# Identity matmuls in two places of the head, and unit 1 as eight plain block products

## The chip, the cores and the metric

The kernel runs on one core of one Trainium2 chip. The metric is the device time of one execution in microseconds, as the median of repeated executions. TensorE multiplies; VectorE, ScalarE and GpSimdE do the elementwise work (GpSimdE does not read PSUM, the buffer in which TensorE sums); SyncE issues nearly all DMAs. In the profile they are PE (and PEld, its weight loads), DVE, ACT, POOL and SP.

## The reference

Packed attention, then a mixture of four experts, all in float32:

```python
scale = 1.0 / np.sqrt(q.shape[-1])
def sm_attn(qq, kk, vv):
    s = scale * np.matmul(qq, kk.transpose(0, 1, 3, 2))
    s = s - np.max(s, axis=-1, keepdims=True)
    a = np.exp(s)
    a = a / (np.sum(a, axis=-1, keepdims=True) + 1e-09)
    return np.matmul(a, vv)
p_packed = sm_attn(p, k, v)            # 8 batches, 8 heads, 32 packed rows of 64
out = sm_attn(q, p_packed, p_packed)   # 576 tokens per batch
...
p = domain_probs / (domain_probs.sum(-1, keepdims=True) + 1e-09)
for e in range(E):                     # 4 experts, x is 4608 x 512
    h = np.maximum(x @ w1[e], 0.0)     # 512 x 1024
    out += p[:, e:e + 1] * (h @ w2[e]) # 1024 x 512
```

## The kernel before

**Precision.** A float32 operand is split into a high part (a cast to the faster float32 format, usually on ScalarE) and a low part (the rest, a subtraction, usually on GpSimdE). A product is three matmuls: high by low, high by high, low by high. `hi_of` and `lo_of` (lines 154 to 160) make the two parts; a low part reads the high part, so it waits for the cast.

**Attention.** `pack_unit` gives the packed rows of a batch and half its heads: scores, softmax, transposes of the softmax by TensorE, the copies of these out of PSUM by ScalarE (tile `at`, lines 247 and 248), the products with v (tile `vt`), and the result `ppbd`. `tok_unit` and, for batch 0, `tok_halves` compute the token side: scores against `ppbd`, softmax on VectorE, and the transposed softmax as `xh` and `xl`. The values are folded into the first expert layer: `g_form` multiplies `ppbd` by w1 (tile `wraw`), and `ghl` is the result's high and low part.

**Experts.** The eight halves of experts (512 of 1024 hidden columns) are chunks. A unit is one batch and one chunk; `units` (line 408) lists 64, of which the first four are (chunk 0, batch 0), (chunk 1, batch 0), (chunk 1, batch 1), (chunk 0, batch 1). Four `mm1_group`s of 12 matmuls make a unit's hidden tiles as four blocks a11, a12, a21, a22 (hidden half by token half); VectorE applies the relu and the probabilities `pbt`. The second layer is a Strassen-like scheme: seven products of 12 matmuls, in the order of `ORDER`, of sums of blocks on the left (`sblk`, `ablk`, their operands `st`, `stl`) and sums of blocks of w2 on the right (`tt`, made by `t_form` from the raw tiles `rw0`, `rw1`). `s_operand` and `split` make the left operands, `product` multiplies and adds into seven accumulators `acc`, and `combine` gives the four output blocks once per batch.

**The head** (lines 686 to 729) interleaves the attention of batches 0 and 1 with chunk 0's `t_form` and unit 0's mm1 groups. Ten identity matmuls open it (`FIRST`), 23 more follow the second mm1 group (`IDLE`); their results are not read. `norm_probs` writes the normalized probabilities to DRAM and `load_probs` reads them back as `pbt`.

**What sets the order.** TensorE's order is fixed by dependencies that `on_pe` and `together` add; in the head `vq` and `gq` do the same for VectorE and GpSimdE, in the order of the code. ScalarE's order, and the rest, is set by a planner at build time, which places each instruction by its own estimate of when it can start; on the chip each engine then takes its instructions in that order. Four PSUM buffers `dbl` and ten `tt` buffers rotate. `t_store` writes the right operands of a chunk to DRAM, `t_load` brings them back.

Of the kernel before, what the change touches and what calls it, by code (L numbers as in the profile page):

```python
# [8 lines left out]
F32 = mybir.dt.float32  # L9
# [7 lines left out]
P = 128  # L17
# [17 lines left out]
ORDER = ["a11", "s3", "s1", "s2", "a22", "s4", "a12"]  # L35
NPROD = len(ORDER)
IDLE = 23
FIRST = 10


@with_exitstack
def attention_moe(ctx: ExitStack, tc: tile.TileContext, q, k, v, p, dp, w1, w2, out):
# [91 lines left out]
    def dbl():  # L134
        return ps_dbl.tile([P, 2, 512], F32, name="dbl")

    ident = const.tile([P, P], F32, name="ident")
# [281 lines left out]
    def split(u, name, psv):  # L419

        tag, bufs = ("stl", 1) if name == "a12" else ("st", 4)
        st = hpool.tile([P, 2, 2, HP], F32R, name=tag, bufs=bufs)[:, :, :, 0:HS]
        hi_of(st[:, 0], psv, nc.scalar)
        lo_of(st[:, 1], psv, st[:, 0], vec)
        blocks[u, "op", ORDER.index(name) if name in ORDER else name] = st

    def mm1_group(u, kh, c, idle=0):
# [35 lines left out]
        )  # L463
        if u == len(units) - 1:
            if c != kh:
                split(u, name, psv)
        elif name == "a21":
            add(held("s3"), blocks[u, "a11"], psv, ALU.subtract)
            add(psv, psv, blocks[u, "a22"], ALU.add)
            add(held("s2"), psv, blocks[u, "a11"], ALU.subtract)  # L470
            nc.scalar.copy(out=held("s1"), in_=psv)  # L471
            if (u, "a12") in blocks:
                add(held("s4"), blocks[u, "a12"], blocks[u, "s2"], ALU.subtract)
        elif name == "a12":
            if (u, "s2") in blocks:
                add(held("s4"), psv, blocks[u, "s2"], ALU.subtract)
            else:
                blocks[u, "a12"] = psv
            split(u, name, psv)
# [32 lines left out]

    def t_form(ch, first=False):

# [4 lines left out]
        }  # L519
        of = {"a11": "b11", "a12": "b21", "s4": "b22", "a22": "t4", "s1": "t1", "s2": "t2", "s3": "t3"}  # L520
        steps = (
            ("a11", "t1", "t3"), ("s3", "s1", "t2"), ("s2", "t4"), ("a22",), ("s4",), ("a12",),
        )
        how = {"t1": ("b12", "b11", "b11"), "t2": ("b22", "t1", "t1"), "t3": ("b22", "b12", "b12"), "t4": ("t2", "b21", "t2")}
        for names in steps:
            for name in names:
                if name in how:
                    continue
                t = wpool.tile([P, 2, 2, DH], F32R, name="tt", bufs=10)
                hi_of(t[:, 0], blk[of[name]], bpool if first and of[name][0] == "t" else bact)  # L530
                tt[ch, ORDER.index(name)] = t
            for name in names:
                if name in how:
                    x, y, place = how[name]
                    bpool.tensor_tensor(out=blk[place], in0=blk[x], in1=blk[y], op=ALU.subtract)
                    blk[name] = blk[place]
                else:
                    t = tt[ch, ORDER.index(name)]
                    lo_of(t[:, 1], blk[of[name]], t[:, 0], bpool)
            yield  # L540

    accs = {}

    def product(u, i):
# [17 lines left out]
        else:  # L562
            vacc.tensor_tensor(out=accs[b, i], in0=psv, in1=accs[b, i], op=ALU.add)

    def store(b, t, r, n, j0=0):
# [20 lines left out]
    def last_unit(u):  # L586

        sb, ch, b = units[u]
        right = {"b11": ORDER.index("a11"), "b21": ORDER.index("a12"), "b22": ORDER.index("s4"), "b12": "b12"}
        pss = {}  # L590
        for half, (left, r) in enumerate((("a11", 0), ("a22", 1), ("a21", 1), ("a12", 0))):
            st = blocks.pop((u, "op", ORDER.index(left) if left in ORDER else left))
            for n in range(2):
                t = tt[ch, right[f"b{left[2]}{n + 1}"]]
                if half < 2:
# [75 lines left out]
    with ExitStack() as first:  # L671
# [26 lines left out]
        raws = w1_load(0)  # L698
        drain(wavefront(packs[:2], 1))
        for i in (2, 3, 2, 3):  # L700
            next(packs[i])
        load_probs(0, 0)
        next(halves)
        vq.on = gq.on = True
        next(forms)
        next(halves)
# [3 lines left out]
        for gen in toks:  # L710
            next(gen)
        load_probs(1, 0)
        for gen in packs[2:]:
# [31 lines left out]
    GROUPS = {1: ((0, 0),), 3: ((1, 1),), 4: ((0, 1),), 6: ((1, 0),)}  # L745
    GROUPS_FIRST = {2: ((0, 0),), 3: ((1, 1),), 4: ((0, 1),), 6: ((1, 0),)}
    GROUPS_LATE = {3: ((0, 0),), 4: ((1, 1),), 5: ((0, 1),), 6: ((1, 0),)}
    FORM = {0: (0, 2, 3, 4, 5, 6), 2: (6,), 3: (0, 1, 2, 3, 4)}
    for kh in range(2):
        w2_load(1, kh, raw_tile)  # L750
    tsteps = nothing
    kind = None
    sums, late, back = nothing, False, second_batch()
    for u, (sb, ch, b) in enumerate(units):
# [23 lines left out]
        if fch is not None and u != 3 and not (u > 3 and odd):  # L778
            tsteps = t_form(fch)
        form_at = FORM.get(u, () if fch is None else (1, 2, 3, 4) if odd else (1, 4))  # L780
# [4 lines left out]
        if u == len(units) - 2:  # L785
            b12_form(ch, raw12)
        for i in range(NPROD):
            product(u, i)
            n = i + LA
            if n < NPROD:  # L790
                s_operand(u, n)
            else:
                n -= NPROD
                s_operand(u + 1, ORDER.index("a22") if n and u == len(units) - 2 else n)
            if i in gat:
# [24 lines left out]
            for _ in range((0, 0, 2, 2, 2, 1, 0)[i] if late else 1):  # L820
                next(sums, None)
            if u < 2 or sb == 0 and u > 3 and not odd:
                t_store(ch, i)
# [48 lines left out]
```

## Time and profile before

| | us |
|---|---|
| median of 3 runs | 1272.03 (1271.49 to 1273.53) |
| span of the profiled execution | 1274.3 |
| TensorE busy | 1255.3 (99%) |
| VectorE / GpSimdE / ScalarE busy | 927.9 / 735.9 / 496.0 |
| mean granted TensorE clock | 0.995 of full |
| start of product 0 of unit 0 | 42.71 |
| start of product 0 of unit 2 | 91.92 |

TensorE's busy time contains matmuls at half the clock and overlapping records, so 99% is not full use. The span runs from the first to the last instruction; the profiled execution's span is longer than the median of the timed runs by 2.3 us. Lines such as L118 and L126 are those of the helpers `mm` and `together`, L70 is that of the recorded VectorE and GpSimdE calls, and L87 and L156 those of ScalarE's copies and casts, so the tile names tell the groups apart.

### The profile page before, as it was taken

What the parts mean: (1) busy time and instruction counts of PE and PEld (TensorE: products, weight loads), DVE (VectorE), ACT (ScalarE), POOL (GpSimd) and SP (SyncE); (2) the same over time, 40 slices, a digit from 0 to 9 for tenths busy, and PEclk for the clock granted to TensorE, in tenths of its full rate; (3) what the DMA queues carried; (4) which work ended last, traced back from release to release, by engine and by line L of the source; (5) the groups of instructions that cost most, each with busy time, mean ns of one, the idle gap of its engine ahead of it and who ended that gap; (6) DMA issues with size and microseconds to landing.
All of it is one profiled execution on the core that took longest, in us unless ns stands there. A gap on an engine that the chain in (4) does not pass through costs nothing.

```text
span 1274.3 us, 27033 instructions
## 1 busy us (share of the span) xinstructions
PE 1255.3 (99%) x10798; PEld 1176.4 (92%) x10798; DVE 927.9 (73%) x1389; ACT 496.0 (39%) x847; POOL 735.9 (58%) x529
## 2 busy tenths in 40 slices
PE   7899999999999999999999999999999999999998
PEld 5789899999999999999999999999999999999998
DVE  6585667788876677788777676788877567767766
ACT  2455444354445243343235433243343533323331
POOL 3876887798684343454467353454557545445456
PEclk8899999999999999999999999999999999999999
DMA  9675665536466444554345555433455443444422
GB/s 328 225 252 195 229 214 203 183 136 204 166 214 214 148 159 131 193 158 166 123 154 177 184 180 174 153 115 126 159 159 178 159 135 116 129 152 159 126 67 75
DMA packets 86508, 213.98 MB, mean 168 GB/s; under 512 B 8816, under 2 KB 27632, under 8 KB 86384
## 3 DMA queue, kind: packets, MB, share of 16 engines
q1 hardware_dynamic: 85712, 212.11, 50.3%
q8 instruction: 86, 1.41, 0.5%
q14 instruction: 38, 0.31, 0.1%
q10 hardware_dynamic: 672, 0.15, 0.1%
HBM read 173.35 MB, written 38.87 MB: 167 GB/s over the span
## 4 chain that ended last, share of the span: by engine, by line
PE 91%; DMA 2%; DVE 2%; POOL 2%; issue 1%; ACT 1%; SPq 0%; DVEq 0%; POOLq 0%; ACTq 0%
PE dbl L118 85%; PE dbl L126 5%; POOL st L70 1%; DMA pnd<-ablk 1%; PE dbl L121 1%; DMA pbt<-pnd 1%; DVE a L70 1%; POOL tt L70 1%; DMA wraw<-in_w 0%; DMA rw<-in_w 0%; DVE dbl L70 0%; DVE sblk L70 0%; POOL acc L70 0%; DVE s L70 0%; POOL rw L70 0%
## 5 line engine op out<-in xcount | busy, mean ns | idle before, releaser
L118 PE MATMUL dbl<-st,tt 128*128 128x288 f32 x4608 | 667.1, 296 | 3.9 <-DVE ghl L70 1.8
L118 PEld LDWEIGHTS dbl<-st,tt 128*128 128x128 f32 x4608 | 624.5, 188 | 38.9 <-POOL st L70 21.2
L70 POOL TENSOR_TENSOR st<-sblk,st 128x576 fp32r<-128x576 f32 x252 | 364.8, 1458 | 438.4 <-ACT st L156 434.1
L118 PE MATMUL dbl<-xh,ghl 128*128 128x288 f32 x2048 | 413.6, 294 | 0.0
L70 DVE TENSOR_TENSOR acc<-dbl,acc 128x576 f32<-128x576 f32 x390 | 292.3, 750 | 92.9 <-PE dbl L118 90.5
L118 PEld LDWEIGHTS dbl<-xh,ghl 128*128 128x128 f32 x2048 | 328.1, 188 | 0.2 <-DVE ghl L70 0.2
L118 PE MATMUL dbl<-xl,ghl 128*128 128x288 f32 x1024 | 302.6, 296 | 2.9 <-POOL xl L70 1.7
L156 ACT CAST st<-sblk 128x576 fp32r<-128x576 f32 x252 | 164.0, 674 | 362.6 <-DVE sblk L70 290.9
L70 POOL TENSOR_TENSOR st<-ablk,st 128x576 fp32r<-128x576 f32 x128 | 187.0, 1461 | 47.8 <-ACT st L156 47.8
L118 PEld LDWEIGHTS dbl<-xl,ghl 128*128 128x128 f32 x1024 | 192.6, 188 | 5.2 <-POOL xl L70 2.6
L70 DVE SCALAR_TENSOR_TENSOR dbl<-dbl,pbt 128x576 f32<-128x576 f32 x128 | 97.8, 764 | 77.0 <-PE dbl L118 75.8
L70 DVE SCALAR_TENSOR_TENSOR ablk<-dbl,pbt 128x576 f32<-128x576 f32 x128 | 96.4, 753 | 66.1 <-PE dbl L118 62.2
L156 ACT CAST st<-ablk 128x576 fp32r<-128x576 f32 x128 | 86.1, 674 | 124.3 <-PE dbl L118 92.4
L118 PE MATMUL dbl<-stl,tt 128*128 128x288 f32 x780 | 114.6, 296 | 0.0
L118 PEld LDWEIGHTS dbl<-stl,tt 128*128 128x128 f32 x780 | 106.0, 188 | 0.2
L70 DVE TENSOR_TENSOR ghl<-dbl,ghl 128x512 fp32r<-128x512 f32 x128 | 85.1, 686 | 27.3 <-ACT ghl L156 27.3
L156 ACT CAST ghl<-dbl 128x512 fp32r<-128x512 f32 x128 | 72.3, 590 | 56.8 <-DVE ghl L70 52.2
L70 POOL TENSOR_TENSOR tt<-rw,tt 128x512 fp32r<-128x512 f32 x57 | 74.3, 1320 | 18.4 <-ACT tt L87 18.4
L70 DVE TENSOR_TENSOR stl<-dbl,stl 128x576 fp32r<-128x576 f32 x64 | 48.4, 756 | 39.5 <-ACT stl L156 39.5
L126 PE MATMUL dbl<-wraw,ppbd 64*32 64x512 f32 x1024 | 68.4, 602 | 3.3 <-DMA wraw<-in_w 3.3
L471 ACT COPY sblk<-dbl 128x576 f32<-128x576 f32 x63 | 40.4, 642 | 64.1 <-DVE sblk L70 64.1
L561 ACT COPY acc<-dbl 128x576 f32<-128x576 f32 x56 | 35.9, 641 | 52.6 <-PE dbl L118 52.5
(68 smaller groups left out, 722.7 us busy)
## 6 DMA issues: line engine op xcount, KB each, us to landing
tt<-td SPq DMA_DIRECT2D x175, 512.0 KB, 4.2
wraw<-in_w SPq DMA_DIRECT2D x132, 256.0 KB, 4.1
td<-tt SPq DMA_DIRECT2D x56, 512.0 KB, 5.4
pbt<-pnd SPq DMA_DIRECT2D x32, 288.0 KB, 4.0
out<-acc SPq DMA_DIRECT2D x31, 288.0 KB, 2.4
rw<-in_w SPq DMA_DIRECT2D x16, 512.0 KB, 5.9
kt<-in_k SPq DMA_DIRECT2D x14, 576.0 KB, 5.5
kt<-in_q SPq DMA_DIRECT2D x14, 576.0 KB, 5.5
```

The costliest lines, as they stand in the source:

```text
L70: res = getattr(self.eng, op)(*args, **kw)
L118: on_pe(nc.tensor.matmul(**kw))
L121: on_pe(nc.tensor.transpose(**kw))
L126: ins = nc.tensor.matmul(**kw).ins
L156: return eng.copy(out=dst, in_=src)
L471: nc.scalar.copy(out=held("s1"), in_=psv)
L561: nc.scalar.copy(out=accs[b, i], in_=psv)
```

## The change

1. `warm` issues n identity matmuls into a spare PSUM tile. Six stand after the third step of the first two `pack_unit`s, 20 after the scores of `tok_halves`.
2. The raw w2 tiles of chunk 1 are loaded in the head, into buffers named `xh1` that batch 1's k tiles have left, instead of after it into `rw0` and `rw1`.
3. Unit 1 no longer uses the seven products. `plain_half` computes the four output blocks as sums of two block products each (`PLAIN`, eight halves of 12 matmuls), both halves of a sum in one PSUM tile; VectorE adds each sum into one or two of the accumulators, so that `combine` stays as it was. Unit 1 then needs the left blocks themselves: a11 and a22 by `s_operand`, a12 and a21 by `split`; and the right blocks b11, b12, b21, b22.
4. `t_form` gets the order `plain`, in which chunk 1's four blocks are made first and the differences t1 to t4, which unit 2 needs, afterwards. The tables that say after which product a step is taken (`FORM`, `GROUPS_FIRST`, `GROUPS_LATE`) follow, and chunk 1's operands are stored in unit 2 instead of unit 1.

```diff
+PLAIN = (
+    ("a11", "b11", 0, 0), ("a12", "b21", 0, 0), ("a11", "b12", 0, 1), ("a12", "b22", 0, 1),
+    ("a21", "b11", 1, 0), ("a22", "b21", 1, 0), ("a21", "b12", 1, 1), ("a22", "b22", 1, 1),
+)
+WARM = (6, 20)
...
+    def warm(out, n):
+        together([dict(out=out, lhsT=ident, rhs=ident, start=True, stop=True) for _ in range(n)])
...
-        tag, bufs = ("stl", 1) if name == "a12" else ("st", 4)
+        tag, bufs = ("stl", 1) if name == "a12" and u != 1 else ("st", 4)
...
-        if u == len(units) - 1:
+        if u in (1, len(units) - 1):
             if c != kh:
                 split(u, name, psv)
...
         steps = (
+            ("b12",), ("a11",), ("s4",), ("a12",), ("t1", "t3"), ("s3",), ("s1", "t2"), ("s2", "t4"), ("a22",),
+        ) if plain else (
             ("a11", "t1", "t3"), ("s3", "s1", "t2"), ("s2", "t4"), ("a22",), ("s4",), ("a12",),
         )
...
+    def plain_half(u, k):
+        sb, ch, b = units[u]
+        left, right, r, n = PLAIN[k]
+        st = blocks[u, "op", ORDER.index(left) if left in ORDER else left]
+        t = tt[ch, RIGHT[right]]
+        if k % 2 == 0:
+            plain["ps"] = dbl()
+        ps = plain["ps"]
+        for j in range(2):
+            k0 = 0
+            for fi in range(2):
+                for tl, sl in ((0, 1), (0, 0), (1, 0)):
+                    mm(
+                        out=ps[:, j, 0:HS], lhsT=t[:, tl, fi, j * P:(j + 1) * P], rhs=st[:, sl, fi, :],
+                        start=k % 2 == 0 and k0 == 0, stop=k % 2 == 1 and k0 == 5,
+                    )
+                    k0 += 1
+        order["product"] = order["free"][-1]
+        if k % 2:
+            psv = ps[:, :, 0:HS]
+            for to, op in {
+                (0, 0): (("a12", ALU.add),), (0, 1): (("s4", ALU.add),),
+                (1, 0): (("a22", ALU.subtract),), (1, 1): (("s3", ALU.add), ("a22", ALU.add)),
+            }[r, n]:
+                acc = accs[b, ORDER.index(to)]
+                vacc.tensor_tensor(out=acc, in0=acc, in1=psv, op=op)
...
-        drain(wavefront(packs[:2], 1))
+        for n, _ in enumerate(wavefront(packs[:2], 1)):
+            if n == 2:
+                warm(dbl()[:, 0, 0:P], WARM[0])
...
         vq.on = gq.on = True
+        warm(dbl()[:, 0, 0:P], WARM[1])
         next(forms)
...
+        for kh in range(2):
+            w2_load(1, kh, lambda shape, name: xpool.tile(shape, F32, name="xh1"))
...
-    FORM = {0: (0, 2, 3, 4, 5, 6), 2: (6,), 3: (0, 1, 2, 3, 4)}
-    for kh in range(2):
-        w2_load(1, kh, raw_tile)
+    FORM = {0: (1, 2, 3, 5), 1: (2, 3, 4, 5, 6), 2: (6,), 3: (0, 1, 2, 3, 4)}
...
-            tsteps = t_form(fch)
+            tsteps = t_form(fch, plain=u == 0)
...
-        for i in range(NPROD):
-            product(u, i)
+        for i in range(NPROD if u != 1 else len(PLAIN)):
+            if u == 1:
+                plain_half(u, i)
+            else:
+                product(u, i)
...
-            if u < 2 or sb == 0 and u > 3 and not odd:
+            if u in (0, 2) or sb == 0 and u > 3 and not odd:
                 t_store(ch, i)
```

What stands in the engines' order as a result is shown at three places. The first is TensorE in pack 0, up to the products with w1 (`a` is the softmax, `vt` the values, `pt` and `ppn` the packed rows). Before:

```order
L126 MATMUL dbl<-kt,pt 32x288 x16
L121 MATMUL dbl<-ident,a_216 128x128 x4
L121 MATMUL dbl<-ident,a_216 64x128
L121 MATMUL dbl<-ident,a_234 128x128 x4
L121 MATMUL dbl<-ident,a_234 64x128
L118 MATMUL dbl<-vt,at 32x64 x40
L121 MATMUL dbl<-ident,ppn 64x128 x2
L126 MATMUL dbl<-st,ppbd_94 32x288 x16
L126 MATMUL dbl<-wraw,ppbd_94 32x512 x8
```

With the change:

```order
L131 MATMUL dbl<-kt,pt 32x288 x16
L126 MATMUL dbl<-ident,a_216 128x128 x4
L126 MATMUL dbl<-ident,a_216 64x128
L131 MATMUL dbl<-ident 128x128 x6
L126 MATMUL dbl<-ident,a_234 128x128 x4
L126 MATMUL dbl<-ident,a_234 64x128
L123 MATMUL dbl<-vt,at 32x64 x40
L126 MATMUL dbl<-ident,ppn 64x128 x2
L131 MATMUL dbl<-st,ppbd_94 32x288 x16
L131 MATMUL dbl<-ident 128x128 x20
L131 MATMUL dbl<-wraw,ppbd_94 32x512 x8
```

The six stand between the transposes of the two halves of the heads, the twenty ahead of the products with w1; nothing else moved there.

The second place is ScalarE at the same time: the copies of the transposed softmax (`at`), the first cast of a raw w2 tile of chunk 0 (`tt<-rw`), and the first Exps of the tokens. Before:

```order
L87 COPY at<-dbl 128x512
L87 COPY at<-dbl 64x128
L87 COPY at<-dbl 128x512
L87 COPY at<-dbl 64x128
L87 CAST tt<-rw_192 128x512
L334 ACTIVATE a_349<-a_349 128x288
```

With the change:

```order
L92 COPY at<-dbl 128x512
L92 COPY at<-dbl 64x128
L92 CAST tt<-rw_192 128x512
L92 COPY at<-dbl 128x512
L92 COPY at<-dbl 64x128
L342 ACTIVATE a_377<-a_377 128x288
```

The cast has moved ahead of the second pair of copies.

The third is GpSimdE from chunk 0's last right operands to the left operands of unit 0 (`rw` and `xh_419`, `xh_421` are raw w2 tiles of chunks 0 and 1; `tt` rows make low parts of right operands, `st` rows low parts of left ones, of which the first is product 1's). Before:

```order
L70 TENSOR_TENSOR tt<-rw_192,tt 128x512
L70 TENSOR_TENSOR rw_192<-rw_192,rw_194 128x2x256
L70 CAST tt<-rw_192 128x512
L70 TENSOR_TENSOR tt<-rw_194,tt 128x512 x2
L70 TENSOR_TENSOR tt<-rw_192,tt 128x512
L70 TENSOR_TENSOR st<-sblk,st 128x2x288 x3
L70 TENSOR_TENSOR st<-ablk,st 128x2x288
```

With the change:

```order
L75 TENSOR_TENSOR tt<-rw_192,tt 128x512
L75 TENSOR_TENSOR rw_192<-rw_192,rw_194 128x2x256
L75 CAST tt<-rw_192 128x512
L75 TENSOR_TENSOR tt<-rw_194,tt 128x512 x2
L75 TENSOR_TENSOR tt<-xh_419,tt 128x512
L75 TENSOR_TENSOR tt<-rw_192,tt 128x512
L75 TENSOR_TENSOR tt<-xh_419,tt 128x512
L75 TENSOR_TENSOR tt<-xh_421,tt 128x512 x2
L75 TENSOR_TENSOR st<-sblk,st 128x2x288 x3
L75 TENSOR_TENSOR st<-ablk,st 128x2x288
```

Four low parts of chunk 1 now stand ahead of product 1's operand.

## Rows read from the trace of the kernel before

**Rows 1.** Windows by stage: us, busy (instructions) by engine, clock, DMA share, GB/s.

```profile
0.00:45.72 45.72, 35.77 (x330) 26.96 (x330) 30.03 (x68) 13.61 (x29) 22.23 (x26) 0.85 0.94 321
45.72:76.04 30.32, 27.09 (x289) 21.79 (x289) 19.41 (x36) 20.23 (x37) 26.09 (x19) 1.00 0.66 238
...
240.00:1274.30 1034.30, 1030.39 (x8696) 978.11 (x8694) 769.83 (x1116) 387.65 (x649) 565.78 (x394) 1.00 0.48 154
```

**Rows 2.** TensorE's waits to 150 us: waited for, total us, times, longest.

```profile
PE dbl L118 <- DVE ghl L70: 1.8, 1, 1.8
PE dbl L118 <- DVE acc L70: 1.8, 1, 1.8
```

**Rows 3.** Windows of the two stretches at the lower clock, as Rows 1.

```profile
18.50:25.00 6.50, 5.54 (x33) 1.94 (x37) 6.23 (x13) 2.07 (x5) 2.86 (x3) 0.50 0.96 333
...
39.00:45.50 6.50, 5.83 (x24) 5.78 (x24) 4.00 (x11) 2.37 (x6) 5.03 (x5) 0.50 0.71 213
```

**Rows 4.** TensorE in time: start, us, operation, records [idle before <-releaser].

```profile
10.83 0.77 PE L121 MATMUL dbl<-ident,a 128*128 128x128 f32 x5 [1.30 <-ACT a L87]
11.52 1.73 PE L118 MATMUL dbl<-vt,at 128*32 128x64 f32 x80
...
13.89 2.29 PE L126 MATMUL dbl<-st,ppbd 64*32 64x288 f32 x32
19.46 4.19 PE L126 MATMUL dbl<-wraw,ppbd 64*32 64x512 f32 x16 [3.29 <-DMA wraw<-in_w]
...
29.49 5.30 PE L126 MATMUL dbl<-ident 128*128 128x128 f32 x46
...
39.66 0.61 PE L118 MATMUL dbl<-xl,ghl 128*128 128x288 f32 x1 [1.05 <-ACT a L87]
...
42.71 3.08 PE L118 MATMUL dbl<-st,tt 128*128 128x288 f32 x12
45.72 1.92 PE L126 MATMUL dbl<-wraw,ppbd 64*32 64x512 f32 x16
...
49.19 1.83 PE L118 MATMUL dbl<-st,tt 128*128 128x288 f32 x12
```

**Rows 5.** ScalarE in order of time, in the columns of Rows 4.

```profile
11.63 0.74 ACT L87 COPY at<-dbl 128x512 f32<-128x512 f32 x2 [0.23 <-PE dbl L121]
15.82 0.62 ACT L87 CAST tt<-rw 128x512 fp32r<-128x512 f32 x1 [3.45 <-DMA rw<-in_w]
...
40.54 0.74 ACT L87 ACTIVATE a<-dbl,nb 128x576 f32<-128x576 f32 x1
```

**Rows 6.** VectorE in order of time, in the columns of Rows 4.

```profile
15.26 0.48 DVE L70 STREAM_TRANSPOSE a<-dbl 128x288 f32<-128x288 f32 x1 [0.78 <-PE dbl L126]
...
24.52 1.25 DVE L70 TENSOR_TENSOR ghl<-dbl,ghl 128x512 fp32r<-128x512 f32 x2
...
29.16 0.76 DVE L70 SCALAR_TENSOR_TENSOR ablk<-dbl,pbt 128x576 f32<-128x576 f32 x1 [1.49 <-DMA pbt<-pnd]
```

**Rows 7.** GpSimdE in order of time, in the columns of Rows 4.

```profile
40.33 3.76 POOL L70 TENSOR_TENSOR tt<-rw,tt 128x512 fp32r<-128x512 f32 x3
47.12 1.41 POOL L70 TENSOR_TENSOR st<-sblk,st 128x576 fp32r<-128x576 f32 x1 [3.03 <-DMA rw<-in_w]
```

**Rows 8.** The chain that ended last, 134 to 145 us: start, us, what.

```profile
134.94 4.93 DMA rw<-in_w
...
139.89 0.62 ACT tt L87
140.51 0.49 ACT ghl L156
```

**Rows 9.** The raw w2 tiles to 60 us: time from DMA issue to landing.

```profile
DMA to landing us min/median/max: 4.6/7.6/9.4
```

**Rows 10.** TensorE in unit 1 and in unit 2, in the columns of Rows 4.

```profile
76.04 4.98 PE L118 MATMUL dbl<-st,tt 128*128 128x288 f32 x36 [1.80 <-DVE acc L70]
...
95.44 0.80 PE L118 MATMUL dbl<-st,tt 128*128 128x288 f32 x4
```

More of the change, by code (lines that the diff above doesn't have):

```diff
@@ L511, in raw_tile, with t_form @@
         return wpool.tile(shape, F32, name=name)
-    def t_form(ch, first=False):
+    def t_form(ch, first=False, plain=False):
         raw = [w2r.pop((ch, kh)) for kh in range(2)]
@@ L519, in t_form @@
         }
-        of = {"a11": "b11", "a12": "b21", "s4": "b22", "a22": "t4", "s1": "t1", "s2": "t2", "s3": "t3"}
+        of = {"b12": "b12", "a11": "b11", "a12": "b21", "s4": "b22", "a22": "t4", "s1": "t1", "s2": "t2", "s3": "t3"}
         steps = (
+            ("b12",), ("a11",), ("s4",), ("a12",), ("t1", "t3"), ("s3",), ("s1", "t2"), ("s2", "t4"), ("a22",),
+        ) if plain else (
             ("a11", "t1", "t3"), ("s3", "s1", "t2"), ("s2", "t4"), ("a22",), ("s4",), ("a12",),
@@ L530, in t_form @@
                 hi_of(t[:, 0], blk[of[name]], bpool if first and of[name][0] == "t" else bact)
-                tt[ch, ORDER.index(name)] = t
+                tt[ch, ORDER.index(name) if name in ORDER else name] = t
             for name in names:
@@ L537, in t_form @@
                 else:
-                    t = tt[ch, ORDER.index(name)]
+                    t = tt[ch, ORDER.index(name) if name in ORDER else name]
                     lo_of(t[:, 1], blk[of[name]], t[:, 0], bpool)
             yield
-    accs = {}
+    accs, plain = {}, {}
+    RIGHT = {"b11": ORDER.index("a11"), "b21": ORDER.index("a12"), "b22": ORDER.index("s4"), "b12": "b12"}
     def product(u, i):
@@ L588, in last_unit @@
         sb, ch, b = units[u]
-        right = {"b11": ORDER.index("a11"), "b21": ORDER.index("a12"), "b22": ORDER.index("s4"), "b12": "b12"}
         pss = {}
@@ L593, in last_unit @@
             for n in range(2):
-                t = tt[ch, right[f"b{left[2]}{n + 1}"]]
+                t = tt[ch, RIGHT[f"b{left[2]}{n + 1}"]]
                 if half < 2:
@@ L745, in attention_moe @@
     GROUPS = {1: ((0, 0),), 3: ((1, 1),), 4: ((0, 1),), 6: ((1, 0),)}
-    GROUPS_FIRST = {2: ((0, 0),), 3: ((1, 1),), 4: ((0, 1),), 6: ((1, 0),)}
-    GROUPS_LATE = {3: ((0, 0),), 4: ((1, 1),), 5: ((0, 1),), 6: ((1, 0),)}
-    FORM = {0: (0, 2, 3, 4, 5, 6), 2: (6,), 3: (0, 1, 2, 3, 4)}
-    for kh in range(2):
-        w2_load(1, kh, raw_tile)
+    GROUPS_FIRST = {2: ((0, 0),), 3: ((1, 0),), 4: ((0, 1),), 6: ((1, 1),)}
+    GROUPS_LATE = {2: ((0, 0),), 4: ((1, 1),), 5: ((0, 1),), 7: ((1, 0),)}
+    FORM = {0: (1, 2, 3, 5), 1: (2, 3, 4, 5, 6), 2: (6,), 3: (0, 1, 2, 3, 4)}
     tsteps = nothing
@@ L786, in attention_moe @@
             b12_form(ch, raw12)
-        for i in range(NPROD):
-            product(u, i)
-            n = i + LA
-            if n < NPROD:
+        for i in range(NPROD if u != 1 else len(PLAIN)):
[3 more added lines that the diff above has]
+                product(u, i)
+            n = i + LA
+            if u == 1:
+                if i == 1:
+                    s_operand(u, ORDER.index("a22"))
+                if n >= len(PLAIN):
+                    s_operand(u + 1, n - len(PLAIN))
+            elif n < NPROD:
                 s_operand(u, n)
@@ L793, in attention_moe @@
                 n -= NPROD
-                s_operand(u + 1, ORDER.index("a22") if n and u == len(units) - 2 else n)
+                if n == 0 or u > 0:
+                    s_operand(u + 1, ORDER.index("a22") if n and u == len(units) - 2 else n)
             if i in gat:
```

## Prediction

> **What bounds the kernel now.** I read the page's table of busy engines first, then stages as windows, then the waits of TensorE, and last each engine's own order of time in the first 80 us. The stages [rows 1] say where anything can be won. From 240 us on TensorE is busy 1030.39 of 1034.30 us at the full clock: that part repeats matmuls, and the change does not touch it. What TensorE loses lies in front: up to 76.04 us it stands idle for 45.72 - 35.77 + 30.32 - 27.09 = 13.2 us, and part of the rest runs at half the clock (0.85 on the mean of the first stage). Two of its waits of 1.8 us each [rows 2] are behind VectorE, one in unit 1 and one near 141 us. Two stretches at the clock's lower level [rows 3] run from 18.5 to 25 us and from 39 to 45.5 us. Ahead of the first TensorE had stood from 16.2 us on (13.89 + 2.29), ahead of the second it was half idle; in both it ran for some 6 us on end before the rise.
>
> But the head is a chain in which TensorE is one of five links, and the reader should follow it from engine to engine: the softmax of batch 0 [rows 4, 5], the scores at 13.89 us, VectorE's token softmax from 15.26 us to the low parts of G at 24.52 us [rows 6], two mm1 groups up to 29.49 us, VectorE's first masked tile at 29.16 us, which waited 1.49 us for the probabilities, the last mm1 group at 39.66 us, and product 0 at 42.71 us. The link that ends last decides, and it is seldom TensorE.
>
> **The change, part by part.**
>
> *The six identity matmuls* stand between the two sets of transposes of pack 0. 23 of the same kind took 5.30 us [rows 4], so one is 0.23 us and six are 1.38 us, in a gap of 1.30 us: 0.1 us by themselves. But ScalarE's order shows what moved with them: the cast of the first w2 tile now stands ahead of the second pair of copies of the transposed softmax, where it stood behind them. That cast began at 15.82 us, after 3.45 us of waiting for its DMA [rows 5]. The copies behind it ran at 11.63 us. The DMA queue is unchanged up to there, so the tile lands when it did. The second pair then starts at 15.82 + 0.62 = 16.4 us and ends 0.74 us later, at 17.2 us instead of 12.4 us: **+4.8 us** on the chain to the scores. That a cast which waits for a w2 tile holds up the casts queued behind it can be seen in this very trace near 140 us [rows 8]: load, cast of w2, cast of G, and TensorE idle for 1.8 us behind VectorE's part of G [rows 2].
>
> *Half clock in that hole.* TensorE then stands from about 12.4 to 17.2 us, longer than the 3.29 us of [rows 4] in which the clock had fallen, so I take the second half of the values products and the first scores at the lower clock. Bounds: nothing, if the clock stays up; at most their full time again, 0.87 us (half of 1.73 us) and 1.37 us (13.89 to 15.26 us). The 16 records on w1 tiles took 4.19 us at the lower and 1.92 us at the full clock [rows 4], near the upper end: I take +1.9 us. VectorE's token softmax starts at 15.26 + 4.8 + 1.9 = 22.0 us.
>
> *The twenty identity matmuls* follow the scores, whose second half took 0.92 us more (to 16.18 us) and takes some 1.8 us at the lower clock: they end near 23.8 us. There is no hole left to fill, since the w1 tiles arrived at 19.46 us. At full clock the twenty take 20 x 0.23 = 4.6 us, on the path (double if the clock is late). The products with w1 run from 28.4 to 30.3 us, a cast (0.62 us, as in [rows 5]) and a low part (1.25 us for two) follow, and the second low part of G is done at 31.6 us, against 25.77 us. VectorE itself would be there 9.3 us after 22.0 us and needs 1.25 us for both, 32.5 us at the latest: the bound is +0.9 us; I stay with 31.6, since some of its operations ran beside GpSimdE's then and do not now. The probabilities landed at 29.1 us, so the wait of 1.49 us is gone; the 29.16 - 1.49 - 25.77 = 1.9 us of VectorE's work in between stays, and the masked tile starts near 33.6 us: **+4.5 us** remain.
>
> *Second stretch at the lower clock.* The 24 matmuls of two mm1 groups (3.2 us) and the 23 old identity matmuls now run to 31.7 + 3.2 + 5.3 = 40.2 us; the Exp that frees PSUM for the last group ends 4.4 us later than 39.66 us, at 44.0 us. TensorE idles about 1.8 us in between instead of 2.8 us, so the clock more likely stays full: group and product 0, 3.05 + 3.01 us [rows 4], would take 1.6 us each, a gain of 2.9 us. Bounds 0 and 2.9; the next step spends it.
>
> *GpSimdE before product 1.* Chunk 1's raw tiles are loaded early and its plain blocks (b12, b11, b22, b21) formed early. Their four low parts now stand on GpSimdE between the last low parts of chunk 0 and the operand of product 1. Before, three low parts ended at 44.09 us, GpSimdE stood 3.03 us, and the operand ran from 47.12 to 48.5 us [rows 7]; that gap covers 3.0 us and no more. Now the casts they need follow both Exps on ScalarE (0.74 us for the second), so the low parts run from about 45.3 us; seven at 1.25 us (3.76 us for three) to 1.3 us make 9.0 us, the operand another 1.4 us: 55.7 us. Product 1 began at 49.19 us and now begins there: **+6.5 us**. With every step above at full clock, without the +1.9 us, the same sum gives 53.8 us, +4.6 us. TensorE idles some 5 us before it, so product 1 and the values products behind it start at the lower clock again, up to 1.6 us more for the product and as much once more before product 2, since ScalarE's copies for it stand behind product 1's eviction: 0 to 3 us, taken as 1.5 us. At product 2 that is **+8 us**, bounds +4.6 and +9.5 us. From there TensorE ran without a wait to 76.04 - 1.80 = 74.2 us, and still will.
>
> *The moved DMAs.* Two 512 KB loads of w2 go to SP's queue behind four w1 loads, ahead of the stores of chunk 0's operands to DRAM. They need the k tiles' buffers, free when batch 1's scores are done, near 32 us. Such loads land in 4.6 to 9.4 us [rows 9], by 44 us if issued by 35 us, before GpSimdE wants them at 47 us: nothing; uncovered it would be GpSimdE's wait, one for one. The stores behind them come later by two issues; nobody reads them back before unit 2: nothing.
>
> *Unit 1.* Eight half sums instead of seven products: 12 matmuls more. 36 took 4.98 us [rows 10] with the last one's tail, 12 are 1.6 us: **+1.6 us**, with TensorE the bound. VectorE loses five operations net, ScalarE and GpSimdE four each: all beside TensorE, worth only the wait they cause, 1.80 us before product 1 of unit 1 [rows 10], which goes, since both halves of a sum share one PSUM buffer: **-1.8 us** (0 if the buffer of the third half is then as late). Next latest there is the operand of a22, formed last; by the same shift it is ready near 83.5 us and wanted near 89 us.
>
> Sum: 8.0 + 1.6 - 1.8 = +7.8 us; as half the terms lean on the clock I take +7.5 us. The profiled execution spans 1274.3 us, 0.2% above the median of 1272.03 us and 0.8 us above the slowest run shown, so its stages stand for the others; I add to the median: 1279.5 us.
>
> **Rivals.**
> 1. *The fill works* (faster). The clock stays full through both stretches. In the first, 2.3 us on the w1 products, VectorE hides it, busy from 15.26 us to its low parts; in the second it is 2.9 us on the path; with 1.8 and 1.6 us of unit 1 that is -3.1 us: 1269 us. It needs the w2 tile to land by about 11.6 us, 4.2 us earlier than it did, while the DMA share of the first stage is 0.94 [rows 1]. 8%. In the Trainium skill, "TensorE: Matmul & The Clock Gate", section "Why this matters for your kernels", asks for matmuls without idle gaps so that the clock stays up; by that rule alone this rival is the outcome. The trace agrees that the clock falls in gaps, but these fillers stand in the same queue as the work.
> 2. *Only ScalarE's displacement bites.* The clock pays back 2.9 of 4.5 us, and GpSimdE's low parts are done by 50 us, from which point on it decides: +1.5 to +4 us, 1273.5 to 1276 us. Against it stand seven low parts in a row. 12%.
> 3. *Chunk 1's differences come late.* The operations that form t1 to t4 now stand on GpSimdE behind unit 1's a22 operand, the last one made; some ten, 13 us, come before the operand of unit 2's second product. From 83.5 us they end near 98 us, and the product is wanted at 95.44 + 7.8 = 103 us [rows 10]. If a22's operand slips past 88 us, unit 2 waits for each us beyond; at 4 us: 1283 to 1287 us. 6%.
>
> **How the numbers follow.** Forecast 74%, 1276.5 to 1281.5 us (the bounds +4.6 and +9.5 us, less 0.2 us). Rivals 8, 12 and 6%. About 0.2%, 2.5 us, is what a measurement of this kernel can tell from no change. Faster: 8% (rival 1). Same: the lower half of rival 2 and a little, 8%. Slower: 84%. A range of 1274 to 1283 us holds the forecast and most of rival 2, some 8 in 10.
>
> **What would show it.** Right: ScalarE's cast of the w2 tile near 15.8 us with the copies behind it; TensorE idle from 12.4 to 17 us and the clock at its lower level before 17 us; product 1 waiting for GpSimdE near 55 us; unit 1 without a wait. Wrong: copies done by 12.5 us (rival 1), product 1 before 51 us (rival 2), or a wait for `st` in unit 2 (rival 3).

## The result, and the profile after

The changed kernel takes 1283.52 us (median of four runs, 1282.58 to 1284.28) against 1271.76 us of the kernel before (now also four runs, 1271.49 to 1273.53): a ratio of 1.0089, with 95% between 1.0075 and 1.0103. It is slower by 11.8 us. Forecast were 1279.5 us and a range up to 1283.0 us: the sign was right, and the size fell 4 us short. One execution of the kernel before (6534 us) and one of a kernel below, e_lowsback (1550 us), both at a mean granted clock far below that of all others (0.18 and 0.75), are left out of every number that follows.

The profiled execution of the changed kernel spans 1281.8 us and was timed at 1283.56 us. The span of the first trace of the kernel before was 1274.3 us. The two traces thus differ by 7.5 us, just what the sum said, while the timed medians differ by 11.8 us. How that can be is the question of the experiments; first the steps, by the rows that answer to those of before.

Windows by stage, in the columns of [rows 1], and two further stretches of the changed kernel:

```profile
0.00:45.72 45.72, 37.84 (x375) 30.35 (x376) 25.76 (x65) 14.00 (x30) 19.25 (x24) 0.93 0.93 328
45.72:76.04 30.32, 24.67 (x241) 20.04 (x240) 12.52 (x24) 11.93 (x23) 14.72 (x12) 0.83 0.49 178
...
17.00:23.00 6.00, 5.94 (x71) 3.33 (x59) 2.55 (x8) 0.30 (x1) 2.92 (x3) 0.50 0.98 344
54.00:65.60 11.60, 9.86 (x111) 8.59 (x112) 0.57 (x2) 2.57 (x5) 6.44 (x5) 0.56 0.40 159
```

The granted clock (the column behind the five engines) is at its lower level, 1.2 GHz, from about 17 to 23 us, and again for most of 54 to 65.6 us. In the first trace of the kernel before, the second of these stretches ran at the full clock.

TensorE's waits to 150 us, in the columns of [rows 2]:

```profile
PE dbl L123 <- POOL st L75: 4.4, 1, 4.4
PE dbl L123 <- ACT at L92: 4.3, 2, 3.5
...
PE dbl L123 <- DVE ghl L75: 1.0, 1, 1.0
```

Two waits are new, one behind ScalarE and one behind GpSimdE; the one on `acc` of [rows 2] is gone. ScalarE in order of time, as [rows 5], says what the first is:

```profile
11.30 0.72 ACT L92 COPY at<-dbl 128x512 f32<-128x512 f32 x2
15.43 0.62 ACT L92 CAST tt<-rw 128x512 fp32r<-128x512 f32 x1 [3.41 <-DMA rw<-in_w]
15.95 0.73 ACT L92 COPY at<-dbl 128x512 f32<-128x512 f32 x2
```

The cast of the first w2 tile stands between the two pairs of copies of the transposed softmax; the second pair waits with it for a DMA that it does not need. GpSimdE in order of time, as [rows 7], says what the second is:

```profile
44.88 2.54 POOL L75 TENSOR_TENSOR tt<-rw,tt 128x512 fp32r<-128x512 f32 x2 [0.71 <-ACT tt L92]
47.37 1.29 POOL L75 TENSOR_TENSOR tt<-xh,tt 128x512 fp32r<-128x512 f32 x1
48.61 1.29 POOL L75 TENSOR_TENSOR tt<-rw,tt 128x512 fp32r<-128x512 f32 x1
49.84 3.73 POOL L75 TENSOR_TENSOR tt<-xh,tt 128x512 fp32r<-128x512 f32 x3
53.52 4.14 POOL L75 TENSOR_TENSOR st<-sblk,st 128x576 fp32r<-128x576 f32 x3
```

Four of seven low parts, those from the `xh` buffers, belong to chunk 1, and only then come the operands `st` for product 1. TensorE in order of time, as [rows 4] and [rows 10]:

```profile
16.58 1.45 PE L123 MATMUL dbl<-vt,at 128*32 128x64 f32 x40 [3.54 <-ACT at L92]
18.79 4.21 PE L131 MATMUL dbl<-st,ppbd 64*32 64x288 f32 x32
22.94 4.95 PE L131 MATMUL dbl<-ident 128*128 128x128 f32 x40
...
34.16 5.30 PE L131 MATMUL dbl<-ident 128*128 128x128 f32 x46
45.18 1.74 PE L123 MATMUL dbl<-st,tt 128*128 128x288 f32 x12
...
54.98 3.25 PE L123 MATMUL dbl<-st,tt 128*128 128x288 f32 x12 [4.42 <-POOL st L75]
62.28 2.66 PE L123 MATMUL dbl<-st,tt 128*128 128x288 f32 x11
...
79.91 1.75 PE L123 MATMUL dbl<-st,tt 128*128 128x288 f32 x12
83.44 5.01 PE L123 MATMUL dbl<-st,tt 128*128 128x288 f32 x36
```

Product 0 (45.18 us) runs at full clock, product 1 (54.98 us) at half: 3.25 us against 1.83 us in [rows 4]. Unit 1 (from 79.91 us) has no wait.

### The profile page after: what moved, and what is told of

It is laid out like the page before. It is cut to its first block, busy times and chain, and to the rows that moved or that the text cites. A ratio compares the mean times of both kernels' runs of the same rounds, so it can differ in the third digit from the quotient of the medians.

```text
span 1281.8 us, 27141 instructions
## 1 busy us (share of the span) xinstructions
PE 1263.3 (99%) x10862; PEld 1185.4 (92%) x10862; DVE 923.9 (72%) x1384; ACT 494.5 (39%) x844; POOL 729.3 (57%) x526
## 4 chain that ended last, share of the span: by engine, by line
PE 93%; POOL 3%; issue 1%; DMA 1%; ACT 1%; DVE 1%; SPq 0%; DVEq 0%; POOLq 0%; ACTq 0%
PE dbl L123 86%; PE dbl L131 7%; POOL st L75 1%; POOL tt L75 1%; DMA rw<-in_w 1%; PE dbl L126 1%; DMA kt<-in_k 0%; POOL acc L75 0%; POOL rw L75 0%; ACT tt L92 0%; ACT ghl L164 0%; DVE dbl L75 0%; DVE ghl L75 0%; ACT st L164 0%; ACT at L92 0%
## 5 line engine op out<-in xcount | busy, mean ns | idle before, releaser
L75 POOL TENSOR_TENSOR st<-sblk,st 128x576 fp32r<-128x576 f32 x248 | 357.7, 1453 | 433.7 <-ACT st L164 424.8
L75 DVE TENSOR_TENSOR acc<-dbl,acc 128x576 f32<-128x576 f32 x383 | 287.0, 750 | 89.3 <-PE dbl L123 86.9
L164 ACT CAST st<-sblk 128x576 fp32r<-128x576 f32 x248 | 161.4, 675 | 359.9 <-DVE sblk L75 281.4
L75 POOL TENSOR_TENSOR tt<-rw,tt 128x512 fp32r<-128x512 f32 x50 | 65.1, 1318 | 17.0 <-ACT tt L92 17.0
```

What stands on the lines that cost most here:

```text
L75: res = getattr(self.eng, op)(*args, **kw)
L164: return eng.copy(out=dst, in_=src)
```

## The experiments

All use the same stations of TensorE, each read from the kernel's own trace (us; "scores" are those of batch 0's first token half, the 23 identities those that were there before; the time is a median, but for b_third and a_again that of one run each):

| kernel | scores | 23 identities | product 0 | product 1 | product 2 | unit 1 | span | time |
|---|---|---|---|---|---|---|---|---|
| before, first trace | 13.89 | 29.49 | 42.71 | 49.19 | 53.39 | 70.65 | 1274.3 | |
| before, again (b_again) | 14.63 | 28.22 | 39.47 | 44.60 | 48.80 | 66.08 | 1269.4 | 1271.47 |
| before, third (b_third) | 14.54 | 28.84 | 40.07 | 45.21 | 49.41 | 66.69 | 1270.0 | 1271.74 |
| after | 18.79 | 34.16 | 45.18 | 54.98 | 61.38 | 79.91 | 1281.8 | 1283.52 |
| after, again (a_again) | 18.68 | 33.40 | 44.42 | 54.22 | 60.62 | 80.38 | 1282.2 | 1284.00 |
| identities alone (e_fillers) | 18.52 | 33.62 | 45.99 | 51.33 | 55.52 | 72.77 | 1275.7 | 1277.04 |
| without identities (e_unit1) | 14.31 | 28.40 | 39.63 | 48.74 | 54.95 | 71.78 | 1274.1 | 1276.17 |
| w2 cast put back (e_castback) | 14.20 | 27.97 | 39.43 | 49.25 | 55.10 | 72.37 | 1274.5 | 1276.42 |
| low parts put back (e_lowsback) | 18.56 | 33.12 | 44.14 | 49.28 | 54.77 | 73.57 | 1275.6 | 1277.37 |
| both put back (e_bothback) | 14.65 | 28.08 | 40.85 | 45.98 | 51.85 | 70.20 | 1272.2 | 1274.01 |
| no identities, low parts put back (e_unit1_lows) | 14.52 | 28.13 | 39.37 | 44.51 | 50.01 | 68.82 | 1271.0 | 1273.17 |
| no identities, three orders put back (e_unit1_at) | 14.21 | 28.35 | 39.60 | 44.74 | 48.94 | 66.21 | 1268.6 | 1270.30 |
| three orders put back (e_all_at) | 14.85 | 28.45 | 41.23 | 46.37 | 50.57 | 67.83 | 1269.8 | 1271.63 |

The last two and a_again were measured later than the others, beside runs of the kernel before with a median of 1272.1 us; for the other experiments it was 1271.6 us. So times of the two groups are compared by their ratio to the runs of before beside them.

**The kernel before, unchanged, once more.**

> The kernel before, unchanged, for a second trace of it. Its first profiled execution spans 1274.3 us, 2.3 us above the median of the timed runs, while that of the changed kernel (1281.8 us) lies 1.8 us below the time of the same execution. Theory A (the first trace was an odd one): this execution spans about 1270 us, and the 4 us lie in the head, where the clock does not fall at 39 us or the stall near 141 us is missing. Theory B (nothing odd): it spans 1274 us again with the clock at its lower level from 18.5 to 25 and from 39 to 45.5 us. Ratio 1.000 in both.

Measured: 1271.47 us against 1271.57 us, ratio 0.9998 [0.9989, 1.0007], and a span of 1269.4 us, 4.9 us under that of the first trace. The windows are those of [rows 3]:

```profile
18.50:25.00 6.50, 5.02 (x47) 1.62 (x46) 6.19 (x16) 2.38 (x5) 2.77 (x4) 1.00 1.07 359
39.00:45.50 6.50, 6.02 (x50) 4.31 (x49) 4.99 (x9) 4.74 (x10) 5.52 (x5) 1.00 0.79 274
```

Both stretches that stood at 0.50 in the first trace run at 1.00 here. The w1 products, which waited 3.29 us for their tiles in [rows 4], wait for 0.58 and 0.34 us:

```profile
17.49 1.05 PE L126 MATMUL dbl<-wraw,ppbd 64*32 64x512 f32 x4 [0.58 <-DMA wraw<-in_w]
18.88 2.47 PE L126 MATMUL dbl<-wraw,ppbd 64*32 64x512 f32 x12 [0.34 <-DMA wraw<-in_w]
```

At product 0 this execution is ahead by 42.71 - 39.47 = 3.24 us, at product 1 by 4.59 us, at the end by 4.9 us: nearly all of it stands by the end of the second stretch. GpSimdE, in the columns of [rows 7], shows another difference:

```profile
38.44 3.79 POOL L70 TENSOR_TENSOR tt<-rw,tt 128x512 fp32r<-128x512 f32 x3
42.53 1.41 POOL L70 TENSOR_TENSOR st<-sblk,st 128x576 fp32r<-128x576 f32 x1 [0.31 <-ACT st L156]
```

The gap ahead of product 1's operand, 3.03 us in [rows 7], is 0.31 us here. So the trace from which the forecast was made was not one of an ordinary execution.

> The kernel before unchanged, one more look. Its first trace showed two stretches at the lower clock and a span of 1274.3 us; its second none and 1269.4 us. Theory A (the first was the exception): span 1269 to 1270, clock 1.00 in the first 76 us. Rival (the execution falls into either with some frequency): a span of 1272 or more and a stretch at half clock near 20 us.

Measured: a span of 1270.0 us, the clock at 1.00 in both windows again, and GpSimdE's gap 0.27 us. In every execution here the time is 1.7 to 1.9 us above the span, so the first trace belongs to an execution of about 1276.1 us, an estimate. The 67 executions of this kernel that were timed in the experiments spread from 1270.32 to 1275.12 us, 24 of them at 1272.5 us or more: the first trace lies beyond the far end of that spread.

**The two halves of the change alone.** Identities: the kernel before and

```diff
+WARM = (6, 20)
...
+            if n == 2:
+                warm(dbl()[:, 0, 0:P], WARM[0])
...
+        warm(dbl()[:, 0, 0:P], WARM[1])
```

> The kernel before with the 6 and 20 identity matmuls alone; unit 1 as before. The cast of the first w2 tile stands ahead of the second copies on ScalarE, as in the change; GpSimdE has no added low parts. Theory (two displacements that add up): the start of product 0 and of the last mm1 group as in the change, near 43.5 to 45.2 us, product 1 near 50.5 us, behind its operand and not 4 us later; time +2 to +6 us, 1274 to 1278 us. Rival (the fillers alone make the loss): +10 us or more, 1282 us. Rival (the fillers do what they are for): 1270 us or less.

Measured: 1277.04 us, ratio 1.0040 [1.0025, 1.0055]. Product 0 comes later than expected, at 45.99 us, since in this trace the mm1 group ahead of it (42.96 to 45.99 us) ran at half clock. ScalarE has the displaced cast here too:

```profile
10.89 0.73 ACT L88 COPY at<-dbl 128x512 f32<-128x512 f32 x2
15.16 0.62 ACT L88 CAST tt<-rw 128x512 fp32r<-128x512 f32 x1 [3.54 <-DMA rw<-in_w]
15.68 0.73 ACT L88 COPY at<-dbl 128x512 f32<-128x512 f32 x2
```

The rest of the change, without the identities:

```diff
-WARM = (6, 20)
+WARM = (0, 0)
```

> The change without its 26 identity matmuls: only the early w2 loads, the early blocks of chunk 1 and the eight half sums. ScalarE's copies stand ahead of the cast again; the four low parts stand ahead of product 1's operand. Theory: product 1 starts at 44.1 + 4 x 1.28 + 1.41 = 50.6 us and some half clock follows; with +1.6 and -1.8 us of unit 1, +2 to +5 us, 1274 to 1277 us. Rival (the low parts are hidden, unit 1 gains by itself): 1270 to 1272 us.

Measured: 1276.17 us, ratio 1.0035 [1.0022, 1.0048]. Product 1 waits for GpSimdE and runs at the lower clock, in a head that is otherwise that of the kernel before:

```profile
48.74 3.25 PE L123 MATMUL dbl<-st,tt 128*128 128x288 f32 x12 [3.61 <-POOL st L75]
```

Apart the halves cost 5.5 and 4.6 us, together 11.8 us. The 1.7 us over their sum lie mostly between product 1 and unit 1: 24.93 us in the changed kernel, 23.04 us without identities, 21.44 us with the identities alone (21.48 us in the kernel before, again). The first two have the wait; behind it the clock stays low to about 64.5 us in the one and 54 us in the other. The identities as such do not explain this: e_castback, next, has all of them and the same wait, and is like the second.

**Each displaced order put back in the whole change.** The cast of the first w2 tile behind both pairs of copies:

```diff
-            bact.copy(out=at[0:r, nfull, :], in_=ps[0:r, 1, 0:P])
+            order["at"] = bact.copy(out=at[0:r, nfull, :], in_=ps[0:r, 1, 0:P]).ins
...
+                if first and name == "a11":
+                    after(res.ins, order["at"])
```

> The whole change, with one order added: ScalarE's cast of the first w2 tile waits in its queue behind both pairs of copies, as before. Theory: the +4.8 us on the chain to the scores is gone, scores at 14 us, VectorE's token softmax at 15.3 us and the mm1 groups near 26 us; the four low parts remain, so product 1 waits until 50 to 52 us: +1 to +5 us, 1273 to 1277 us. Rival (the twenty fillers are what delays the head): mm1 groups near 28 us or later and 1280 us or more.

Measured: 1276.42 us, ratio 1.0038 [1.0024, 1.0053]. All 26 identities are there, and the scores and product 0 (39.43 us) begin as in the kernel before; the wait for GpSimdE is left:

```profile
14.20 2.29 PE L131 MATMUL dbl<-st,ppbd 64*32 64x288 f32 x32
...
49.25 3.25 PE L123 MATMUL dbl<-st,tt 128*128 128x288 f32 x12 [4.43 <-POOL st L75]
```

Of its own the identity work costs nothing that can be measured here (the kernel without it took 1276.17 us); what it cost was the cast that the planner moved across it. The order of chunk 1's casts and low parts behind the casts and low parts of the left operands, from unit 0 instead of from unit 1:

```diff
     tsteps = nothing
+    bact.on = bpool.on = True
```

> The whole change, but chunk 1's plain blocks give way in unit 0: their casts and low parts stand behind the casts and low parts of the left operands on ScalarE and GpSimdE. The cast of the w2 tile stays ahead of the second copies of the softmax. Theory A (the change costs two separate things in the head, ScalarE's displaced cast and GpSimdE's four low parts, and the low clock that each gap brings): product 1 no longer waits for GpSimdE behind seven low parts, and begins near 51 us, as in the kernel with the identities alone; the time is that kernel's 1277.0 less the 0.3 us that unit 1 gains, 1276.0 to 1277.5. Theory B (the four low parts are needed soon anyway, so that moving them only moves the wait to products 3 to 6 of unit 0 or into unit 1): product 1 early, but a wait for GpSimdE of 2 us or more in front of a later product, 1279 or more.

Measured: 1277.37 us, ratio 1.0042 [1.0029, 1.0055], and product 1 at full clock without a wait:

```profile
49.28 1.83 PE L123 MATMUL dbl<-st,tt 128*128 128x288 f32 x12
```

That is the upper edge of A, and B's later wait for GpSimdE did not come. Both orders put back together:

> The whole change with both orders put back: the w2 cast behind both pairs of softmax copies, chunk 1's casts and low parts behind the left operands. The 26 identity matmuls and the eight plain block products stay. Theory A: nothing of the cost is left; product 0 near 39.4 us (the twenty identities are covered, as with the cast put back alone), product 1 near 44.6 us, unit 1 0.3 us shorter: 1271.0 to 1271.6, against 1271.6 of the kernel before. Theory B (the identities themselves cost, 26 x 0.23 us of which some part is on the path): 1273 or more. Theory C (the identities win something over the kernel before, since the clock stays up): 1270 or less.

Measured: 1274.01 us, ratio 1.0016 [1.0006, 1.0026]. A missed (1271.0 to 1271.6 us), and the time lies in B's range, in which the identities themselves cost. And this without the identities, WARM at (0, 0) and the line with `bact.on`:

> The change without the 26 identity matmuls, and with chunk 1's casts and low parts behind the left operands. Theory A: product 1 near 44.6 us as before, unit 1 0.3 us shorter, 1271.0 to 1271.6; so the identities are worth nothing either way beside the kernel with both orders put back. Theory B (the low parts only move their wait): 1273 to 1276.

Measured: 1273.17 us, ratio 1.0018 [1.0008, 1.0027]. There are no identities here, so most of what was left is not theirs. A missed again, and B has the time but not the reason: TensorE does not wait for GpSimdE. Something that I had not seen was left, between product 1 (44.51 us, in time) and product 2 (50.01 us, 1.2 us late). ScalarE shows it:

```profile
45.99 0.64 ACT L92 CAST tt<-xh 128x512 fp32r<-128x512 f32 x1
46.52 0.75 ACT L92 COPY at<-dbl 128x512 f32<-128x512 f32 x2
...
48.25 0.64 ACT L92 CAST tt<-xh 128x512 fp32r<-128x512 f32 x1
48.77 0.76 ACT L92 COPY at<-dbl 128x512 f32<-128x512 f32 x2
```

It is the first displacement over again: casts of chunk 1's blocks stand ahead of the copies of *batch 1's* transposed softmax, for which TensorE waits (0.83 and 1.34 us here), and product 2 behind them then ran at half clock, 2.88 us for 11 matmuls instead of 1.72 us. The changed kernel does not pay this: there the four casts are done at 48.1 us, before TensorE begins, at 49.25 us, the transposes whose result these copies take. It is the line with `bact.on` that moved the casts back to where they meet the copies; e_lowsback, which has no other edit, shows them there too (53.02 us, the copies at 53.54 us).

**The third order put back as well.** Chunk 1's casts behind batch 1's copies, and its steps two products later:

```diff
-    FORM = {0: (1, 2, 3, 5), 1: (2, 3, 4, 5, 6), 2: (6,), 3: (0, 1, 2, 3, 4)}
+    FORM = {0: (3, 4, 5, 6), 1: (2, 3, 4, 5, 6), 2: (6,), 3: (0, 1, 2, 3, 4)}
...
+                if plain or first and name == "a11":
+                    after(res.ins, order["at"])
```

> As the kernel without identities and with chunk 1's blocks behind the left operands, and besides ScalarE's casts of chunk 1's plain blocks stand behind the copies of batch 1's transposed softmax (in the previous run two stood ahead of the first pair of these copies and one ahead of the second; product 2 began at 50.01 us against 48.80 us in the kernel before and then ran at half clock). Theory A (these three casts are all that is left of the cost): product 2 near 48.8 us at full clock, unit 1 without its wait of 1.8 us, 1271.0 to 1271.6 us against 1271.6 us of the kernel before. Theory B (unit 1 or the moved loads cost something of their own further on): still 1272.5 or more with product 2 early.

Measured: 1270.30 us, ratio 0.9989 [0.9979, 0.9998]: with unit 1 in plain products and nothing displaced the kernel is a shade faster than before, by 0.1%, which the interval just tells from nothing. Theory B is out; the places are those of A, the time a little under its range. Product 2 begins at 48.94 us and runs at full clock, and TensorE has no wait in unit 1.

```profile
48.94 0.40 PE L123 MATMUL dbl<-st,tt 128*128 128x288 f32 x1
...
49.52 1.72 PE L123 MATMUL dbl<-st,tt 128*128 128x288 f32 x11
```

The same edit in the whole change, identities and all:

> The whole change with all three orders put back: the w2 cast behind the copies of batch 0's softmax, chunk 1's casts behind those of batch 1's, chunk 1's low parts behind the left operands. The 26 identities and the eight plain block products are left. Theory A (the identities are covered when nothing is displaced): 1271.0 to 1272.0 us. Theory B (the identities cost by themselves through the order around the scores of batch 1, where the run with two orders put back had a stretch at half clock from 37.9 us and product 0 at 40.85 us instead of 39.4 us): product 0 again after 40.5 us and 1272.5 to 1273.5 us. Theory C (they win): 1270 or less.

Measured: 1271.63 us, ratio 0.9996 [0.9987, 1.0005]; the identities do not win, and here they come out 1.3 us longer than without them. The time is that of theory A, the place that of theory B, product 0 at 41.23 us. The twelve matmuls of the mm1 group ahead of product 0 run at half clock after waits of 1.50 and 1.04 us:

```profile
35.71 0.40 PE L123 MATMUL dbl<-xl,ghl 128*128 128x288 f32 x1 [1.50 <-POOL xl L75]
...
38.21 0.61 PE L123 MATMUL dbl<-xl,ghl 128*128 128x288 f32 x1 [1.04 <-ACT a L92]
38.62 0.68 PE L123 MATMUL dbl<-xh,ghl 128*128 128x288 f32 x2
39.10 0.44 PE L123 MATMUL dbl<-xl,ghl 128*128 128x288 f32 x1
```

Without the identities the same group takes 39.60 - 37.91 = 1.69 us at full clock, with them 41.23 - 38.21 = 3.02 us: 1.33 us, as much as the two kernels differ. This does not come with the identities each time: in e_castback, with the same waits of 1.50 and 1.05 us, the group ran at full clock. Before this place nothing was won: VectorE begins the low parts of G at 24.17 us without and at 24.27 us with the identities, and the 23 identities begin at 28.35 and 28.45 us.

**The changed kernel once more.**

> The changed kernel once more, unchanged. Theory A (its stretches at half clock near 17 to 23 us and 54 to 65 us follow from its two gaps): both again, span 1281 to 1283 us, scores near 18.8 us and product 1 near 55 us. Rival (the clock falls by chance, as it did in the first trace of the kernel before): one of the two is missing and the span is 1279 us or less.

Measured: 1284.00 us, a span of 1282.2 us, both stretches at the lower clock again, product 1 with its wait of 4.42 us and 3.25 us. In all executions of the changed kernel the mean clock is 0.992 or 0.993 of full, in those of the kernel before 0.995 to 1.000. The changed kernel's two low stretches come with its two waits, in both traces; without the first wait the first is gone (e_castback), and without both waits both are (e_all_at). Those of the first trace of before came with one execution.

## Why the prediction was right and wrong

**Wrong: the last line of the sum.** "The profiled execution spans 1274.3 us, 0.2% above the median of 1272.03 us and 0.8 us above the slowest run shown, so its stages stand for the others; I add to the median." Its stages did not stand for the others. The steps were costed against a head that contained two stretches at half clock, and these were gone in the second and third trace, with 4.9 and 4.3 us. Against these the change costs 12.4 and 11.8 us of span. The step that carried the error into the sum is "Product 1 began at 49.19 us and now begins there: +6.5 us": the 54.98 us that were measured for it are near the forecast, but in the other two traces product 1 of the kernel before began at 44.60 and 45.21 us. Two credits of the sum are of the first execution alone. It let TensorE win back 2.9 us in the second stretch, which the others do not have to give, and it let GpSimdE's gap of 3.03 us cover as much of the four low parts, where the others have 0.31 and 0.27 us. Two signs were in the material: the span alone was above the slowest run shown (with the 1.8 us that only the later runs show it is 1276.1 us, 2.6 us above), and exactly the stages on which the sum rested held the only half-clock stretches of the trace. The same sum set on its own execution, 1274.3 + 7.5 + 1.8 = 1283.6 us, is what was measured (1283.52 us). That it agrees to 0.1 us is luck: as the next paragraphs show, the half clock behind product 1 cost 2.0 us more than was taken for it, and an earlier product 1 (0.7 us) and a gain behind unit 2 (1.5 us) made up for it.

**Right: ScalarE's displaced cast.** Forecast were the second copies at 16.4 us and +4.8 us at the scores; they came at 15.95 us and the scores 4.90 us later (18.79 against 13.89 us). e_castback shows that it is the cast: with it back the scores stand at 14.20 us.

**Right: half clock in that hole, +1.9 us.** The values products behind the wait took 1.45 us for half of the 1.73 us that they took together in [rows 4], and the scores 4.21 us for 2.29 us; VectorE's token softmax began at 21.14 us (forecast 22.0) and, as its second half waits for the scores, its masked tile at 33.17 us (forecast 33.6), without the wait for the probabilities.

**Right: the twenty on the path, while the cast is displaced.** They ran from 22.94 to 27.8 us, w1 products behind them. e_castback adds what the sum could not tell: when the cast is not displaced they cost nothing at product 0 (39.43 us there, 39.47 and 40.07 us in the second and third trace of before).

**Right: the second stretch avoided.** The last mm1 group and product 0 at full clock, the latter 1.74 us against 3.08 us in [rows 4].

**Right: four low parts ahead of product 1's operand.** Forecast 55.7 us, measured 54.98 us; e_lowsback and e_unit1 show it alone.

**Mis-sized: the half clock behind it.** Taken as 1.5 us, bounds 0 and 3. Product 1 to product 2 took 6.40 us against 4.20 us before, product 2 to unit 1 18.53 us against 17.26 us: 3.5 us, since the clock came back only near 64.5 us. Of this 1.3 us lie behind product 2, for which the sum had nothing ("From there TensorE ran without a wait [...] and still will"). Product 1 was 0.7 us earlier than forecast, and so product 2 stood at +8.0 us as forecast, but unit 1 at +9.3 us. The cover came later and was not forecast: behind unit 2 the changed kernel is shorter by 1.5 us, of which 0.8 us are the wait near 141 us [rows 2] that shrank from 1.82 to 1.01 us; 0.4 us lie in unit 2 and 0.3 us behind the wait, and why is not settled.

**Right: unit 1 and the moved loads.** 12 matmuls more against the wait on `acc`: from unit 1's first product to unit 2's 21.01 us against 21.27 us, -0.26 us (forecast -0.2). In the changed kernel no row waits for the moved w2 loads.

**The rivals.** Rival 1 (the fill works): not in any run. The Trainium skill, "TensorE: Matmul & The Clock Gate", section "Why this matters for your kernels", asks for matmuls without idle gaps. The runs agree in part: behind 4.42 us product 1 ran at 0.50, while behind shorter gaps the clock fell in some traces and not in others. But the head without the 26 identities had the clock at 1.00 anyway (b_again), and even with all orders put back they gained nothing that can be measured. Rival 2: wrong for the whole change; e_fillers and e_lowsback, in which the low parts do not hold up product 1, come nearest to it: 5.5 and 5.3 us against the runs of before, but 1.4 and 1.3 us of span against the first trace, on which its 1.5 to 4 us were worked out. Both have a further stretch at half clock of their own. Rival 3: no wait for `st` in unit 2 of the changed kernel.

**Not foreseen, but no cost of the changed kernel:** chunk 1's casts ahead of batch 1's softmax copies on ScalarE. In the changed kernel they hold nothing up; where the second order was put back they did. Moved behind the copies, and the steps that form the blocks two products later, they were worth 2.5 and 3.7 us (ratios 1.0016 to 0.9996, and 1.0018 to 0.9989); which of the two edits gave how much was not separated.

## What to carry to other kernels

Before a sum of stages is added to a median, add the time around the span and see where the profiled execution lies among the timed runs; where the stages of the sum hold low-clock stretches, cost them at full clock as well, and give the difference to the range. Work put into a gap must be judged by what the planner moves across it: here the added matmuls themselves cost between nothing that can be measured (e_castback) and 1.3 us (e_all_at), and the cast and the low parts that changed places, with the half clock behind the waits they made, nearly all of the 11.8 us. A cast that waits for a DMA belongs behind everything on its engine that is ready and wanted.

## What the runs showed of the hardware

One and the same program ran its head with two stretches at half clock (18.5 to 25 and 39 to 45.5 us) and, in two other traces, with none, a difference of 4.3 to 4.9 us in 1270. The wait for the w1 tiles was 3.29 us in the first, 0.92 us together in the second, and 1.80 us in the third. The second stretch is not explained by its waits. The mm1 group behind the Exp came after a wait of 1.04 to 1.11 us in all these kernels. It ran at half clock in the first trace of before and in e_fillers, e_bothback and e_all_at, and at full clock in the nine other traces. Some 2.5 us ahead stood another wait, of 1.50 us in the first trace of before, in e_bothback and in e_all_at; but e_castback has 1.50 us as well and ran at full clock, and e_fillers has 0.64 us and ran at half. What decides between the cases stays open.

Behind the 4.42 us wait the clock did not come back with the work: the changed kernel's TensorE was busy for 9.86 of 11.60 us, at 0.56 of full clock on the mean, and in the repeat for 10.62 us at 0.50. The length of the wait does not set this: behind 4.43 us in e_castback, with TensorE busy from 49.25 us on, the clock was back at full by 54 us.
